# Loading a quarter of each query block first, and a highway pass by 128-column chunks, in a top-32 attention kernel

## The chip, the cores and the metric

The kernel runs on one core of a Trainium2 chip. The metric is the device time of one execution in microseconds; the median of three runs before the change is 874.89 us (874.78 to 874.94).

The core's engines work side by side, each through its own list of instructions in order, and wait for each other by semaphores: PE (matrix multiplication and transposes), DVE (vector work, here the search for the largest scores), ACT (activations and copies out of PSUM), POOL (vector work on SBUF) and SP (which issues most transfers). PE writes to PSUM, which has 8 banks of 512 fp32 columns; SBUF holds everything else.

## The reference, cut to what matters

```python
# q, k, v: batch 8, 8 heads, sequence 576, head dimension 64, float32
scores = scale * np.matmul(q, k.transpose(0, 1, 3, 2))
kth = np.partition(scores, -32, axis=-1)[..., -32:-31]
scores = np.where(scores >= kth, scores, -1e9)
attn = np.exp(scores - scores.max(-1, keepdims=True))
attn = attn / (attn.sum(-1, keepdims=True) + 1e-9)
x = np.matmul(attn, v)            # then heads side by side: 4608 rows of 512
H = np.maximum(x @ w_h, 0.0)      # highway pass
T = 1.0 / (1.0 + np.exp(-(x @ w_t + b_t)))
out = T * H + (1.0 - T) * x
```

Each of the 36,864 score rows (8 x 8 x 576) of 576 elements keeps its 32 largest.

## The kernel before

**Tiles and groups.** The 576 rows of a head are cut into four interleaved quarters of 128 (row 4p + j is row p of quarter j) and a rest of 64. A group is one quarter (or the rests) of all 8 heads of a batch; it holds four pairs of tiles, each 128 query rows by 576 scores of two heads (the rest: two pairs of four heads). There are 144 pairs in all. Batch 0 starts with its quarter 0, heads 0 and 1.

**One pair's way.** `scores` (L186) multiplies the transposed queries with the transposed keys into the PSUM tile `ps` of four banks, of which there is one. `evac` (L206) lets ACT write relu(ps) into `z`. `tree` (L217) lets DVE take `hi`, the larger of each two of the 576 scores: the first half is read from `ps`, the second from `z`, so `ps` is free for the next pair only when `hi` is done. After each second pair, `folds` (L232) halves `hi` into `hh` and `h`, and `minima` (L252) lets POOL keep the smaller ones. `lists` and `lists_rest` (L338, L352) find the 32nd largest with DVE's MAX8 and MATCH_REPLACE8, the bulk of its work. `mask` (L376) lets ACT write a penalty `pen` for all scores below that; `parts` (L425) lets PE transpose scores and penalty into `zt` (four 128-chunks of one head) and `zr` (the last chunk of both heads, made by `ends`), and ACT take the exponential `et`; `av` (L456) multiplies by the values and ACT copies the sums out as `xs`. `norm` (L490) divides.

**Highway pass.** Per group, `ffn_x` transposes x into `xT`, `ffn_h` and `ffn_t` multiply with the two weights, and DVE, POOL and accumulating transfers combine the results.

**Order.** The main loop (L892) goes over steps n: `tree(n)`, folds after odd n, mask of pair n - 4, values of pair n - 5, scores of pair n + 1, lists. The engines' instructions are pinned to this written order (`Pinned`, L25); so are the DMAs issued with `ops.nc.queue`, while those issued with `nc.sync` are placed on SP's queue by a scheduler. The preparation of the next batch (its loads and transposes, `begin`, L802) is spread over the steps from 17 pairs before its first.

**The opening (L832 to L856).** For each pair of heads hp, `load` (L105) brings a block of keys `kin` and one of queries `qin`, all four quarters, in two transfers of 128 KB; `load_rest` (L116) brings the rests of all heads. `turn` (L138) transposes a block with four PE transposes into a PSUM bank `kqps` and copies it to `kq`, on ACT or, where `vec` is set, on DVE. Banks come from `ztps` (two) or from `fps` (one, tag "fp"). `turn_rest` (L157) does the same for the rests. Before scores(0) come: 12 idle transposes (`spin`), turn of kin 0, 3 spins, turn of qin 0 (copied by DVE), turn_rest of pair 0. In steps 0 to 2, the blocks hp = n + 1 are turned before scores(n + 1). DVE so has the copies of q blocks 0 and 1 among its first four instructions.

**The end (L979 to L1025).** Below, m is the third pair from the end, gp the group before the last, gl the last. The end is written out by hand: gp's highway pass, transposes and exponentials of pairs m + 1 and m + 2, then `values(m + 1)`, the last `zt`, and `values(m + 2)`. Then the highway pass of gl: one reciprocal over all heads and x in two halves (`norm`), four transposes and `xT` in two halves (`final_x`), `ffn_h` (hps), `ffn_d`, the judge, and `final_t` and `final_o` in two halves of 256 columns. The judge (L865 to L880) reduces flags that say whether a slower exact path has to run: `judge_lists` and `judge_scales` over the whole kernel's lists and reciprocals, `judge` over the partitions, by a PE transpose `bps`.

Of the kernel before, what the change touches and what calls it, by code (L numbers as in the profile page):

```python
# [8 lines left out]
AF = mybir.ActivationFunctionType  # L9
ALU = mybir.AluOpType  # L10
# [57 lines left out]
class Ops:  # L68
# [36 lines left out]
    def load(self, pr, name, hp, eng=None, other=None):  # L105
        nc, D, P = self.nc, self.D, self.P
        eng = eng or nc.sync
        t = self.ldpool.tile([P, J, 2, D], FP32, tag=name, name=name)
        src = pr[name[0]](2 * hp, 2 * hp + 2, 0, J * P)
        for hh in range(2):  # L110
            (other if other and hh else eng).dma_start(
                t[:, :, hh, :], src[hh].rearrange("(p j) d -> p j d", j=J)
            )
        pr[name, hp] = t

    def load_rest(self, pr, name, eng=None):  # L116
        t = self.ldpool.tile([self.R, self.H, self.D], FP32, tag=name, name=name, bufs=1)
        (eng or self.nc.sync).dma_start(
            t[:], pr[name[0]](0, self.H, J * self.P, self.S).rearrange("h p d -> p h d")
        )  # L120
        pr[name] = t
# [16 lines left out]
    def turn(self, pr, name, hp, bank=None, vec=False):  # L138


        nc, P = self.nc, self.P
        t = pr.pop((name, hp))
        pool, tag = (self.ztps, "zt") if bank else (self.fps, "fp")
        kqps = pool.tile([P, 512], FP32, tag=tag, name="kqps")
        for c in range(J):
            nc.tensor.transpose(
                kqps[:, c * P : (c + 1) * P],
                t[:, c, :, :].rearrange("p h d -> p (h d)"),
                self.ident[:],
            )  # L150
        dst = pr["kq"][:, "kq".index(name[0]), hp, 0 : J * P]
        if vec:
            nc.vector.tensor_copy(dst, kqps[:])
        else:
            nc.scalar.copy(dst, kqps[:])

    def turn_rest(self, pr, h0, h1):  # L157


        nc, R = self.nc, self.R  # L160
        kqps = self.fps.tile([self.P, 512], FP32, tag="fp", name="kqps")
        view = kqps[:].rearrange("p (i h r) -> p i h r", i=2, r=R)
        for i, name in enumerate(("krest", "qrest")):
            for hp in range(h0, h1):
                nc.tensor.transpose(
                    view[:, i, hp, :],
                    pr[name][:, 2 * hp : 2 * hp + 2, :].rearrange("p h d -> p (h d)"),
                    self.ident[0:R, 0:R],
                )
        nc.scalar.copy(  # L170
            pr["kq"][:, :, h0:h1, J * self.P : self.S], view[:, :, h0:h1, :]
        )
# [44 lines left out]
    def tree(self, n):  # L217
# [3 lines left out]
        if n % 2 == 0:  # L221
# [5 lines left out]
        ps = self.st[n].pop("ps")  # L227
        nc.vector.tensor_tensor(
            hi[:, half, :], ps[:, :, 0:H1], self.st[n]["sc"][:, :, H1:S], ALU.max
# [271 lines left out]
    def norm_x(self, g):  # L501
# [8 lines left out]
        for hs in (slice(0, H // 2), slice(H // 2, H)) if g.final else (slice(0, H),):  # L510
            made = (nc.vector if g.final else nc.gpsimd).tensor_tensor(
                x3[:, hs, :],
                xs3[:, hs, 0:D],
                rinv[0:ql, hs].unsqueeze(2).to_broadcast([ql, hs.stop - hs.start, D]),
                ALU.mult,
            )
# [6 lines left out]
    def final_x(self, g):  # L523


        nc, P, n_g = self.nc, self.P, self.n_g
        g.xT = self.fpool.tile([P, n_g, P], BF16, tag="xT", name="xT")
        g.xh = self.fpool.tile([P, self.dm], FP32, tag="xh", name="xh")
        half = n_g // 2
        for i0 in (0, half):  # L530
            xtps = self.ztps.tile([P, 512], FP32, tag="zt", name="xtps")
            for i in range(half):
                nc.tensor.transpose(
                    xtps[:, i * P : (i + 1) * P],
                    g.x[:, (i0 + i) * P : (i0 + i + 1) * P],
                    self.ident[:],
                )
            src = xtps[:, 0 : half * P].rearrange("p (g j) -> p g j", j=P)
            dst = g.xT[:, i0 : i0 + half, :]
            if i0:  # L540
                nc.scalar.mul(dst, src, 0.5)
            else:
                nc.vector.tensor_scalar_mul(dst, src, 0.5)
        nc.scalar.mul(g.xh[:], g.x[:], -0.5)

    def final_t(self, g, banks):
# [4 lines left out]
        g.tp = [b[:, 0:W] for b in banks]  # L551
        for j, tp in enumerate(g.tp):
            cs = slice(j * W, (j + 1) * W)
            for i in range(n_g):
                nc.tensor.matmul(
                    tp, g.xT[:, i, :], self.wt[:, i, cs],
                    start=(i == 0), stop=False,
                )
            nc.tensor.matmul(
                tp, self.cst[:], self.bt[:, cs], start=False, stop=True  # L560
            )
            nc.scalar.activation(tp, tp, AF.Tanh)
# [126 lines left out]
def kernel(  # L689
# [65 lines left out]
    with ExitStack() as cm:  # L755
# [78 lines left out]
        for name in ("kin", "qin"):  # L834
            ops.load(pr, name, 0, queue, nc.scalar)
        for name in ("krest", "qrest"):
            ops.load_rest(pr, name, queue)
        for hp in (1, 2):
            for name in ("kin", "qin"):
                ops.load(pr, name, hp, queue)  # L840
# [8 lines left out]
        spin(3)  # L849
        ops.turn(pr, "qin", 0, True, True)  # L850
        ops.turn_rest(pr, 0, 1)
        for name in ("kin", "qin"):
            ops.load(pr, name, 3, queue)
        ops.load_values(pr, queue)
        ops.scores(0, *pairs[0], preps[0])
        ops.evac(0)  # L856
        ffn = []
        step = 0
        ok = const([P, 4], FP32, "ok")
        bad = const([P, 4], FP32, "bad")  # L860
# [10 lines left out]
        def judge_scales():  # L871
            vec.tensor_reduce(ok[:, 2:3], scales[:], op=ALU.min, axis=AX.XY)
            vec.tensor_scalar(bad[:, 2:3], ok[:, 2:3], FAINT, None, ALU.is_lt)
            vec.tensor_reduce(bad[:, 3:4], bad[:, 0:3], op=ALU.max, axis=AX.X)

        def judge():
            bps = ops.zrps.tile([P, 512], FP32, tag="zr", name="bps")
            ops.nc.tensor.transpose(bps[0:1, 0:P], bad[:, 3:4], ident[:])
# [13 lines left out]
        while step <= NPR:  # L892
            n = step
            if have(n):
# [3 lines left out]
                if n + 1 < NHP:  # L898
                    for name in ("kin", "qin"):
                        ops.turn(  # L900
                            pr, name, n + 1, True, n == 0 and name == "qin"
                        )
                    if n == 0:
                        ops.turn_rest(pr, 1, NHP)
# [95 lines left out]
        ops.ffn_d(gp, ops.ffn_t(gp))  # L1000
        part, ends = ops.parts(m + 1)
# [4 lines left out]
        ends()  # L1006
        part, ends = ops.parts(m + 2, banks[3])
        part(0)
        ends()
        ops.ffn_e(gp)  # L1010
        ops.ffn_o(gp, *out_rows(gp))
        values(m + 1)
        part(1)
        judge_lists()
        values(m + 2)
        ops.norm(gl)
        ops.final_x(gl)
        judge_scales()
        ops.spare = [ops.fps.tile([P, 512], FP32, tag="fp", name="hps")]
        ops.ffn_h(gl)  # L1020
        ops.ffn_r(gl)
        ops.ffn_d(gl)
        judge()
        ops.final_t(gl, banks[0:2])
# [76 lines left out]
```

## Time and profile before

| | us |
|---|---|
| median of 3 runs | 874.89 |
| the profiled execution, its own time | 874.66 |
| its span, from the first instruction to the last | 872.9 |
| DVE busy | 843.6 |
| PE busy | 707.8 |
| ACT busy | 695.9 |
| POOL busy | 690.8 |
| first hi of DVE starts | 10.56 |
| second hi starts | 14.55 |
| first fold (hh) starts | 15.35 |
| last list maximum of DVE starts (two of them, 0.56) | 853.97 |
| last xs copied | 861.18 |
| last o of the highway pass ends | 868.23 |

How to read it: an engine's list is one line per instruction or run of like instructions: start, duration, engine, line, operation, what is written from what, count, and in brackets how long the engine was idle before it and whose end let it go on. All kernel instructions that go through `Pinned` show its line, L35, so they are told apart by the names of their tiles. The chain of waits follows the last instruction back to what released it. DVE's instructions and their waits decide here; the granted clock of PE is given as a share of full speed.

### The profile page before, as it was taken

To read this page: it belongs to the slowest core of one execution; us is meant where nothing else is said; L and a number is where in the kernel's file an instruction comes from. 1 tells how busy PE (TensorE), PEld (TensorE's weight loads), DVE (VectorE), ACT (ScalarE), POOL (GpSimd) and SP (SyncE) were. 2 spreads that over 40 slices of the span, in tenths; PEclk is the share of its full clock that TensorE was granted. 3 is DMA by queue.
4 is the path that set the end of the run, shared out by engine and by line. 5 is a ranking of instruction groups with operands and counts; after the bars stand their busy time and mean duration, and the time that the engine had idled before them with its cause. 6 is when DMAs were issued, how large, how long until landed. Compare 5 with 4: busy or idle time off the path is not lost.

```text
span 872.9 us, 19884 instructions
## 1 busy us (share of the span) xinstructions
PE 707.8 (81%) x6569; PEld 500.4 (57%) x6569; DVE 843.6 (97%) x4200; ACT 695.9 (80%) x1244; POOL 690.8 (79%) x447
## 2 busy tenths in 40 slices
PE   6777988879788788778788798887978878887975
PEld 5455655655565555655565565665556655555653
DVE  4999999999999999999999999999999999999995
ACT  3788878888788887888888887888878888677784
POOL 5788887888878888888888888878888888877880
PEclk9799999999999998999999999999989999899898
DMA  9553422234234331323323432323412111111111
GB/s 196 130 110 62 109 38 57 60 62 98 37 62 92 73 86 29 70 67 62 86 50 56 96 80 56 62 64 69 105 37 46 42 37 38 37 26 25 26 39 38
DMA packets 104494, 57.06 MB, mean 65 GB/s; under 512 B 82112, under 2 KB 91712, under 8 KB 104384
## 3 DMA queue, kind: packets, MB, share of 16 engines
q1 hardware_dynamic: 92768, 37.37, 17.0%
q0 software_dynamic: 10416, 17.96, 13.6%
q8 instruction: 53, 0.87, 0.4%
q14 instruction: 57, 0.47, 0.2%
q10 hardware_dynamic: 1200, 0.39, 0.2%
HBM read 30.67 MB, written 17.30 MB: 55 GB/s over the span
## 4 chain that ended last, share of the span: by engine, by line
DVE 90%; PE 4%; POOL 2%; DMA 1%; issue 1%; ACT 1%; SPq 0%; DVEq 0%; POOLq 0%; ACTq 0%
DVE w L35 48%; DVE m L35 18%; DVE hi L35 11%; DVE hh L35 6%; DVE h L35 4%; DVE d L35 3%; PE ps L35 1%; POOL hi L35 1%; PE zt L35 1%; POOL hh L35 1%; PE t L35 1%; DMA d<-xh 1%; DMA qrest<-in_q_dram 1%; PE zr L35 1%; ACT z L35 1%
## 5 line engine op out<-in xcount | busy, mean ns | idle before, releaser
L35 PE MATMUL ps<-kq 64*128 64x64 f32 (+3 forms) x1280 | 212.1, 457 | 89.5 <-DVE hi L35 85.4
L35 ACT ACTIVATE z<-ps 128x1152 f32<-128x1152 f32 x144 | 163.0, 1132 | 103.5 <-PE ps L35 101.2
L35 ACT ACTIVATE pen<-z,m 128x576 bf16<-128x576 f32 x288 | 225.9, 785 | 1.3 <-DVE m L35 1.1
L35 PE MATMUL zt<-ident,z 128*128 128x128 f32 x1152 | 225.7, 289 | 0.1
L35 PE MATMUL zt<-nident,pen 128*128 128x128 bf16 x1152 | 215.0, 225 | 0.3 <-ACT pen L35 0.3
L35 PEld LDWEIGHTS ps<-kq 64*128 64x128 f32 (+1 forms) x1280 | 107.5, 184 | 187.6 <-DVE hi L35 96.1
L35 POOL TENSOR_TENSOR hi<-z,hi 128x1152 int32<-128x1152 int32 x72 | 189.3, 2630 | 14.7 <-DVE m L35 9.2
L35 POOL TENSOR_TENSOR hh<-hi,hh 128x576 int32<-128x576 int32 x71 | 100.2, 1411 | 126.3 <-DVE w L35 126.3
L35 POOL TENSOR_TENSOR hi<-hi,z 128x1152 int32<-128x1152 int32 x72 | 190.3, 2643 | 5.7
L35 PEld LDWEIGHTS zt<-ident,z 128*128 128x128 f32 x1152 | 169.9, 147 | 19.1 <-ACT xT L35 0.6
L35 ACT ACTIVATE et<-zt 128x512 bf16<-128x512 f32 x288 | 161.5, 606 | 14.1 <-PE zt L35 13.3
L35 PEld LDWEIGHTS <-pen 128*128 128x128 bf16 x1440 | 160.0, 111 | 1.7 <-ACT pen L35 1.7
L35 DVE MAX8 m<-w 128x8 f32<-128x168 f32 x576 | 160.4, 320 | 0.0
L35 DVE MAX8 w<-hi 128x8 f32<-128x288 f32 x288 | 116.7, 447 | 0.0
L35 DVE TENSOR_TENSOR hi<-ps,z 128x576 f32<-128x576 f32 x144 | 106.8, 741 | 6.5 <-ACT z L35 6.5
L35 PE MATMUL zr<-v,et 128*128 128x65 bf16 (+1 forms) x1590 | 89.6, 196 | 18.5 <-ACT et L35 14.6
L35 POOL TENSOR_TENSOR hh<-hh,hi 128x576 int32<-128x576 int32 x71 | 100.0, 1408 | 5.6
L35 PEld LDWEIGHTS <-et 128*128 128x128 bf16 (+1 forms) x1600 | 69.8, 101 | 60.0 <-ACT et L35 46.0
L35 DVE MATCH_REPLACE8 w<-m,w 128x168 f32<-128x168 f32 x288 | 89.4, 318 | 0.0
L35 DVE MAX8 w<-hh 128x8 f32<-128x72 f32 x576 | 84.3, 221 | 0.0
L35 PE MATMUL zr<-ident,z 128*128 128x128 f32 x286 | 74.2, 313 | 3.5 <-ACT xs L35 3.5
L35 PE MATMUL zr<-nident,pen 128*128 128x128 bf16 x286 | 59.8, 230 | 0.3 <-ACT pen L35 0.3
(91 smaller groups left out, 1111.6 us busy)
## 6 DMA issues: line engine op xcount, KB each, us to landing
vin<-in_v_dram SPq DMA_DIRECT2D x8, 1024.0 KB, 5.6
kin<-in_k_dram SPq DMA_DIRECT2D x63, 128.0 KB, 3.4
qin<-in_q_dram SPq DMA_DIRECT2D x63, 128.0 KB, 3.1
out_dram<-x SPq DMA_DIRECT2D x30, 256.0 KB, 2.8
d<-xh POOLq DMA_DIRECT2D x30, 256.0 KB, 3.8
out_dram<-d POOLq DMA_DIRECT2D x30, 256.0 KB, 4.4
krest<-in_k_dram SPq DMA_DIRECT2D x8, 128.0 KB, 4.2
qrest<-in_q_dram SPq DMA_DIRECT2D x8, 128.0 KB, 5.0
```

What stands on the lines that cost most here:

```text
L35: return self._tc.keep_in_program_order(fn(*args, **kw))
```

## The change

There are three parts.

1. **Opening.** Scores of the first group need only quarter 0 of each query block. A new `load_first` brings that quarter for heads 0 and 1, and then for heads 2 to 7, into a tile `qc`; `turn_first` transposes it (one transpose per pair of heads) and DVE copies it to `kq`. The rest of the query blocks is loaded later, without that quarter (`c0=1`), and turned in steps 3 to 6, on the single fps bank with ACT copies of 128x384; the query rests are loaded from step 4 and turned in step 8. `krest` comes in two pieces, the first on ACT's queue. Keys are turned one step earlier: kin 1 before the first step, and kin n + 2 in step n, ahead of scores(n + 1) on PE and ACT. The 3 spins are gone. As the q blocks share three buffers, and the query rests one, with those of batch 1, SP's order of loads changes: the query rest of batch 1 is now loaded before that of batch 0.
2. **First maxima.** For the first four pairs `tree` reads both operands from `z`; `ps` is free when ACT has evacuated it.
3. **End.** The highway pass of the last group runs in column chunks as pairs of heads end: chunks 0 and 1 (heads 0 to 3) are normalised and transposed while gp's pass and the last pairs are still at work, chunks 2 and 3 follow one by one, and hps and the two t tiles accumulate chunk by chunk, with the bias first. The scaled copy `xh` goes to POOL but for the last chunk. The last `zt` goes ahead of `values(m + 1)`. `judge_scales` comes early and `judge_last` checks the last group's reciprocals.

The diff, cut to its core:

```diff
-    def load(self, pr, name, hp, eng=None, other=None):
+    def load(self, pr, name, hp, eng=None, other=None, c0=0):
...
-                t[:, :, hh, :], src[hh].rearrange("(p j) d -> p j d", j=J)
+                t[:, c0:J, hh, :],
+                src[hh].rearrange("(p j) d -> p j d", j=J)[:, c0:J, :],
...
+    def load_first(self, pr, eng, h0, h1):
+        if not h0:
+            pr["qc"] = self.ldpool.tile(
+                [self.P, self.H, self.D], FP32, tag="qc", name="qc", bufs=1
+            )
+        src = pr["q"](h0, h1, 0, J * self.P)
+        eng.dma_start(
+            pr["qc"][:, h0:h1, :],
+            src.rearrange("h (p j) d -> p h j d", j=J)[:, :, 0, :],
+        )
+
+    def turn_first(self, pr, h0, h1):
+        nc, P = self.nc, self.P
+        kqps = self.ztps.tile([P, 512], FP32, tag="zt", name="kqps")
+        for hp in range(h0, h1):
+            nc.tensor.transpose(
+                kqps[:, hp * P : (hp + 1) * P],
+                pr["qc"][:, 2 * hp : 2 * hp + 2, :].rearrange("p h d -> p (h d)"),
+                self.ident[:],
+            )
+        nc.vector.tensor_copy(
+            pr["kq"][:, 1, h0:h1, 0:P],
+            kqps[:, h0 * P : h1 * P].rearrange("p (h q) -> p h q", q=P),
+        )
...
-    def turn(self, pr, name, hp, bank=None, vec=False):
+    def turn(self, pr, name, hp, bank=None, c0=0):
...
-        for c in range(J):
+        for c in range(c0, J):
...
-        ps = self.st[n].pop("ps")
+        ps, sc = self.st[n].pop("ps"), self.st[n]["sc"]
+        if n < 4:
+            ps = sc
         nc.vector.tensor_tensor(
-            hi[:, half, :], ps[:, :, 0:H1], self.st[n]["sc"][:, :, H1:S], ALU.max
+            hi[:, half, :], ps[:, :, 0:H1], sc[:, :, H1:S], ALU.max
         )
...
+    def final_norm(self, g, i0, i1):
+        nc, P, D = self.nc, self.P, self.D
+        hs = slice(2 * i0, 2 * i1)
+        xs3 = g.xs[:].rearrange("p (h e) -> p h e", e=D + 1)
+        rinv = self.scales[:, g.gi, hs]
+        nc.vector.reciprocal(rinv, xs3[:, hs, D])
+        nc.vector.tensor_tensor(
+            g.x[:].rearrange("p (h d) -> p h d", d=D)[:, hs, :],
+            xs3[:, hs, 0:D],
+            rinv.unsqueeze(2).to_broadcast([P, 2 * (i1 - i0), D]),
+            ALU.mult,
+        )
+
+    def final_turn(self, g, i0, i1, xtps):
+        nc, P = self.nc, self.P
+        for i in range(i0, i1):
+            nc.tensor.transpose(
+                xtps[:, (i - i0) * P : (i - i0 + 1) * P],
+                g.x[:, i * P : (i + 1) * P],
+                self.ident[:],
+            )
...
+        if i1 - i0 == 1 and i1 < self.n_g:
+            nc.scalar.mul(dst, src, 0.5)
+        else:
+            nc.vector.tensor_scalar_mul(dst, src, 0.5)
+        if i1 == self.n_g:
+            nc.scalar.mul(g.xh[:, cs], g.x[:, cs], -0.5)
+        else:
+            nc.gpsimd.tensor_scalar_mul(g.xh[:, cs], g.x[:, cs], -0.5)
...
-        for name in ("kin", "qin"):
-            ops.load(pr, name, 0, queue, nc.scalar)
-        for name in ("krest", "qrest"):
-            ops.load_rest(pr, name, queue)
-        for hp in (1, 2):
-            for name in ("kin", "qin"):
-                ops.load(pr, name, hp, queue)
+        ops.load(pr, "kin", 0, queue, nc.scalar)
+        ops.load_rest(pr, "krest", nc.scalar, 0, 2)
+        ops.load_first(pr, queue, 0, 2)
+        ops.load(pr, "kin", 1, queue)
+        ops.load_first(pr, queue, 2, H)
+        ops.load_rest(pr, "krest", queue, 2, H)
+        ops.load(pr, "kin", 2, queue)
...
         spin(12)
         ops.turn(pr, "kin", 0, True)
-        spin(3)
-        ops.turn(pr, "qin", 0, True, True)
-        ops.turn_rest(pr, 0, 1)
-        for name in ("kin", "qin"):
-            ops.load(pr, name, 3, queue)
+        ops.turn_first(pr, 0, 1)
+        ops.turn_rest(pr, 0, 1, ("krest",))
+        ops.load(pr, "kin", 3, queue)
+        ops.load(pr, "qin", 0, queue, None, 1)
         ops.load_values(pr, queue)
+        ops.load(pr, "qin", 1, queue, None, 1)
+        ops.load(pr, "qin", 2, queue, None, 1)
         ops.scores(0, *pairs[0], preps[0])
         ops.evac(0)
+        ops.turn_first(pr, 1, NHP)
+        ops.turn(pr, "kin", 1, True)
+        ops.turn_rest(pr, 1, NHP, ("krest",))
...
-                if n + 1 < NHP:
-                    for name in ("kin", "qin"):
-                        ops.turn(
-                            pr, name, n + 1, True, n == 0 and name == "qin"
-                        )
-                    if n == 0:
-                        ops.turn_rest(pr, 1, NHP)
+                if n + 2 < NHP:
+                    ops.turn(pr, "kin", n + 2, True)
+                if NHP <= n + 1 < 2 * NHP:
+                    ops.turn(pr, "qin", n + 1 - NHP, None, 1)
+                if n == NHP:
+                    ops.load(pr, "qin", 3, None, None, 1)
+                    ops.load_rest(pr, "qrest")
+                if n == 2 * NHP:
+                    ops.turn_rest(pr, 0, NHP, ("qrest",))
...
         ops.ffn_d(gp, ops.ffn_t(gp))
+        ops.final_begin(
+            gl, ops.fps.tile([P, 512], FP32, tag="fp", name="hps"), banks[1:3]
+        )
...
+        ops.final_norm(gl, 0, 2)
+        ops.ffn_e(gp)
+        ops.ffn_o(gp, *out_rows(gp))
+        ops.final_turn(gl, 0, 2, banks[0])
         part, ends = ops.parts(m + 2, banks[3])
         part(0)
         ends()
-        ops.ffn_e(gp)
-        ops.ffn_o(gp, *out_rows(gp))
+        judge_lists()
+        judge_scales()
+        part(1)
         values(m + 1)
-        part(1)
-        judge_lists()
+        ops.final_norm(gl, 2, 3)
         values(m + 2)
-        ops.norm(gl)
-        ops.final_x(gl)
-        judge_scales()
-        ops.spare = [ops.fps.tile([P, 512], FP32, tag="fp", name="hps")]
-        ops.ffn_h(gl)
-        ops.ffn_r(gl)
+        ops.final_h(gl, 0, 2)
+        ops.final_turn(gl, 2, 3, ...)
+        ops.final_norm(gl, 3, 4)
+        ops.final_t(gl, 0, 2)
+        ops.final_turn(gl, 3, 4, ...)
+        ops.final_h(gl, 2, 3)
+        ops.final_t(gl, 2, 3)
+        judge_last(gl)
+        ops.final_h(gl, 3, 4)
         ops.ffn_d(gl)
+        ops.final_t(gl, 3, 4)
         judge()
-        ops.final_t(gl, banks[0:2])
         ops.final_o(gl, out_rows(gl), (nc.sync, ops.nc.scalar))
```

`final_h` and `final_t` are `ffn_h` and the old `final_t` for chunks i0 to i1; `final_t` puts the bias matmul first and the tanh after the last chunk.

## The prediction

> **What bounds the kernel now.** I read the page's busy line and slices first, then what DVE waited for, then the opening and the tail instruction by instruction.
>
> ```profile
> PE 707.8 (81%) x6569; PEld 500.4 (57%) x6569; DVE 843.6 (97%) x4200; ACT 695.9 (80%) x1244; POOL 690.8 (79%) x447
> DVE  4999999999999999999999999999999999999995
> ```
>
> DVE is busy 97%, at 9 in every slice but the first and the last. So 29.3 us (872.9 - 843.6) is all that any change can win without taking work off DVE, and it should lie at the ends. The waits of DVE say where:
>
> ```profile
> DVE kq L35 <- PE kqps L35: 7.2, 1, 7.2
> DVE hi L35 <- ACT z L35: 6.5, 4, 2.6
> DVE scales L35 <- ACT xs L35: 2.8, 1, 2.8
> ```
>
> 7.2 us before the first copy, 6.5 us before first maxima (hi), 2.8 us before the last reciprocal. Between 60 and 850 us the same view has one wait of 0.4 us. Now the opening, from the timeline:
>
> ```profile
> 8.06 1.30 PE L35 MATMUL ps<-kq 64*128 64x512 f32 x8
> 9.39 1.13 ACT L35 ACTIVATE z<-ps 128x1152 f32<-128x1152 f32 x1 [0.91 <-PE ps L35]
> 10.56 0.76 DVE L35 TENSOR_TENSOR hi<-ps,z 128x576 f32<-128x576 f32 x1 [2.64 <-ACT z L35]
> ...
> 12.06 1.30 PE L35 MATMUL ps<-kq 64*128 64x512 f32 x8 [0.71 <-DVE kq L35]
> ...
> 14.55 0.76 DVE L35 TENSOR_TENSOR hi<-ps,z 128x576 f32<-128x576 f32 x1 [2.64 <-ACT z L35]
> 15.35 0.76 DVE L35 TENSOR_TENSOR hh<-hi 128x576 f32<-128x576 f32 x1
> ```
>
> From 15.35 DVE runs without a gap, but for 0.84 us before the fourth hi (23.05). So the opening is worth what the start of the folds (hh, 15.35) moves, plus that 0.84. Scores(0) waits for qrest (issued 3.09, landed 4.8 later, 7.89); scores(1) waits for DVE's copy of the second q block (11.23 to 11.91), which stands behind the first hi. The tail, from the chain of waits:
>
> ```profile
> 859.14 0.73 PE zt L35 x8
> 859.87 0.02 issue
> 859.89 0.60 ACT et L35
> ...
> 860.91 0.28 ACT xs L35
> ...
> 861.58 0.43 DVE x L35
> ...
> 863.08 1.48 PE hps L35 x4
> 864.55 0.21 PE bps L35
> 864.77 2.15 PE t L35 x10
> ...
> 867.80 0.43 DVE o L35
> ```
>
> From the last xs (ends 861.18) to the last o (ends 868.23) lie 7.05 us of serial highway pass in one piece. After it the store and the program's end take 4.7 us, which nothing here changes.
>
> **The opening, part by part.** Loads: all these DMAs move 256-byte pieces, and the issues with their times to landing give the rate: the first half of k block 1 landed at 8.27 (3.77 + 4.5) as byte 896 KB of the queue, the first half of q block 2 at 11.86 (7.96 + 3.9) as 1664 KB, so 214 GB/s, 0.6 us per 128 KB; early ones were 256 KB by 4.16 (k block 0) and 512 KB by 6.22 (q block 0). I place the new order on this line by cumulated bytes: k block 0 4.16 as before; with the first qc piece (64 KB) and krest of two heads (32 KB, on ACT's queue, same bytes) 352 KB: 4.16 + 96/256 x 2.06 = 4.9 to 5.7; k block 1 (608 KB) 6.8; other qc (800 KB) 8.0; other krest (896 KB) 8.3; k block 2 (1152 KB) 9.5; qrest of batch 1, which SP now issues here, 1280 KB; k block 3 (1536 KB) 11.3; the rest of q block 0 12.2; vin some 4 us later, about 17 instead of 19.3.[...]
>
> Scores(0): k block 0 is transposed 4.26 to 5.35 as before; then one qc transpose and one krest, 0.27 each: 5.9 to 6.2; DVE's 128x128 copy, between 0.2 and the 0.69 of the 512-wide one, takes about 0.3 and ACT's 64-wide one 0.2 (0.27 at 128): scores(0) at 6.3 for 8.06. With the 1.30 to 1.6 for them, z(0) runs 7.8 to 8.95. DVE must then copy the other qc (landed 8.0, three transposes to 8.45, copy 0.55 by 384/512 of 0.69) to 9.05 before the first hi, which so starts at 9.1. That copy is a new thing in front of hi, but z(0) hides all but 0.1 of it.
>
> Scores(1) now stands behind k blocks 1 and 2 on PE: block 2 landed 9.5, four transposes 0.66: 10.2. ACT's copies in front of it (k block 1 from 9.1, 0.58; krest, 0.35) end 10.1. It no longer waits for hi(0), as ps is free when z(0) ends. Scores(1) 10.2 to 11.5, z(1) to 12.7, hi(1) to 13.5: folds at 13.5, **1.85 us earlier**. hi from z instead of ps costs nothing: 128x576 takes 0.758 from SBUF (hh<-hi) and 0.741 from ps.
>
> Then z(2) is ready at 15.8 and DVE wants it at 17.15 (13.5 + 3.67 as now). Scores(3) starts when z(2) ends (15.9) instead of when hi(2) ends (19.9); even in 2.40 us z(3) ends 19.45, wanted at 20.35: the **0.84 us** go too.
>
> **What is moved into the steady part.** Steps 3 to 6 each get three transposes (0.5 on PE) and a 128x384 ACT copy (0.45), step 8 the qrest turn (0.4 PE, 0.3 ACT). All use the single fp bank, so from step 5 on PE waits there until ACT has copied batch 1's block out (35.40 to 35.98 for the first), and values(0) and the next scores queue behind it: 0.7 wait + 0.45 + 0.5 put z(6) about 1.1 later. Now z(5), z(6), z(7) end 1.14, 1.63 and 2.19 us before hi wants them (34.34, 40.13, 45.64). That fits, narrowly; below it costs nothing, above, with PE slow, up to 1.2. I take 0.3. The qrest load waits for batch 1's turn_rest (one buffer): issued about 44.2, landed 47.4, PE there about 47.5, hi(8) 48.7, so hidden with some 2 us to spare.
>
> **The tail, part by part** (times as if the rest stood still). Heads 0 to 3 are complete with the xs at 854.66: reciprocal 0.2 and x 0.42 on DVE after 855.12, in the 0.67 us in which DVE now waits for the tanh; PE's two transposes at 856.7 (0.4), while it waits for pen until 857.23; xT (0.42) to 857.6. Free. xh goes to POOL: 1.27 for a 512-wide pair op bounds it above; POOL is idle from 857.97 and xh is wanted at 863, so any price hides.
> The judge's reductions (1.80 + 0.27 + 0.48 + 0.15) follow on DVE to 860.3, where it now idles to 861.21.
> Values(m+1) go behind the last zt on PE: zt starts at 858.45 instead of 858.94, and xs(m+1) leaves ACT's path, so et ends 859.95 (860.49) and the last xs 860.7 (861.18): 0.5 gained. DVE: pair 2's reciprocal 860.3, x (its 0.17 gap, then 0.28 for 128 columns, between 0.2 and 0.42) to 860.95; pair 3's to 861.6.
> PE: two hps (0.52 of the 1.04 that four take at full clock) to 861.0; transpose; six 256-wide t at 0.13 to 862.05; last transpose to 862.3; chunk 2's three 0.52; xT of chunk 3 on DVE (0.28) to 862.65; its hps 863.0 and t 863.3. DVE: judge_last (three small ones and gaps, 0.6; two of them are new) 863.25; d 0.69; flag 0.45 to 864.4; then d, o, d, o of 0.42 each with gaps, ending 866.18 instead of 868.23. **2.05 us.** Fully at half clock PE's part is 1.2 longer: 0.9.
>
> **The clock speaks against parts of this.** The windows:
>
> ```profile
> 20.00:25.00 5.00, 2.99 (x12) 1.64 (x14) 4.09 (x22) 1.13 (x1) 3.15 (x2) 0.54 0.84 175
> 863.00:866.00 3.00, 2.92 (x12) 1.68 (x13) 1.74 (x7) 0.90 (x3) 0.00 (x0) 0.59 0.00 0
> ```
>
> Granted 0.54 and 0.59: in the first the same scores took 2.39 for 1.30, in the second four hps 1.48 for 1.04. The Trainium skill (TensorE: Matmul & The Clock Gate, "What's actually happening") says that full clock is granted only after a free-running window of some 3.4 us found PE busy, and is lost after an idle one. By that rule, taking 3 spins and four q blocks' transposes from the opening makes PE idler and could leave it slow sooner or longer: scores(0) at half clock puts the folds 0.6 to 1.1 later (gain 0.75 to 1.25), and a slow window over scores(6) brings out the 1.2. By the rows, 12 spins and k block 0 fill PE from 1.59 on as now; z(2) and z(3) have 0.9 to spare at half clock. I go with the rows, and let the rule set the 0.3 and the upper end. In the tail the rule favours the change: PE has less idle time between 860 and 863.
>
> **Sum.** Span 872.9 - 1.85 - 0.84 + 0.3 - 2.05 = 868.5. The profiled execution took 874.66, 1.76 over its span: 870.2. It lies 0.23 under the median 874.89: **870.4 us**, 0.5% faster.
>
> **Rivals.**
> (a) The steady part eats the opening: the fp bank and a slow window make z(6) and z(7) late, 1.2 and about 0.8. For it: the 1.14 and 1.63 us of slack. Against: DVE lost nothing at 25 to 60 us even with 2.4 us scores. 872.1.
> (b) The tail stays serial: PE at half clock through it, or DVE's judge work (to 860.3) holding pair 2 back: gain 0.9 instead of 2.05: 871.5. For it: DVE has only 0.3 us of slack there.
> (c) It does nothing at the start, qc landing as late as qrest did (7.9): the folds move by 0.3 only, the 0.84 stays won: 872.0. Against: it is byte 352 KB, not 768.
> (d) Slower: PE loses the full clock in the opening and does not get it back. At half clock its 4.8 us of a 5.8 us step become 9 or so, PE is the bound, and every window of 3.4 us costs DVE some 1.3 to 1.7. It decides from the third window beyond today's four slow ones (20.4 to 34.1); five are slower by 0.2%: 877. Against: the second slice of the whole span and all later ones show 0.9 and above after the same sparse opening.
>
> **How the numbers follow.** A measurement of this kernel tells about 0.2% (1.75 us) from no change. Forecast as summed 0.58, own range 869.3 to 871.3; (a) 0.14, (b) 0.13, (c) 0.06, (d) 0.04, and 0.05 for a gain larger than forecast (all best ends: folds 2.3, tail 2.6: 869.0). Low 868.9 takes the last; high 872.6 takes (a), (b), (c) with their spread, leaving (d) and two rivals together. Same needs 873.1 or more, two rivals at once: 0.06; slower 0.04; faster 0.90.
>
> **What would show it.** Right: first hi near 9.1, folds near 13.5, no DVE wait before the fourth hi, hi without waits at 25 to 60 us, last o some 5.5 us after the last xs, which comes 0.5 nearer to the last list maximum. Wrong: DVE hi waiting for ACT z at 30 to 50 us with PE at kqps before it; granted clock 0.5 in more than four windows before 40 us; PE waiting for qc beyond 6; d of the last group waiting for hps or xh beyond 863.3.

## The result: no difference, and the profile after

| | before | after |
|---|---|---|
| median, same chip, us | 874.84 (4 runs, 874.04 to 874.94) | 875.65 (4 runs, 874.83 to 876.04) |
| ratio, 95% interval | | 1.001 (0.9993 to 1.0027) |
| profiled execution, us | 874.66 | 875.56 |
| its span, us | 872.9 | 873.7 |

The forecast was 870.4 us, 868.9 to 872.6. The change made the kernel neither faster nor slower. Both ends did gain, though. The table cuts the two spans at the same events, taken from the timelines (starts of DVE's instructions; the ends of the last xs and the last o):

| stretch, us | before | after | difference | predicted |
|---|---|---|---|---|
| start to first fold (hh) | 15.35 | 13.04 | -2.31 | -1.85 |
| first fold (hh) to fifth hi | 13.49 | 13.95 | +0.46 | -0.84 |
| fifth to eleventh hi | 34.00 | 39.88 | +5.88 | +0.3 |
| eleventh hi to last list maximum | 791.13 | 790.36 | -0.77 | 0 |
| to the last xs | 7.20 | 6.79 | -0.41 | -0.5 |
| to the last o | 7.05 | 4.81 | -2.24 | -1.55 |
| to the end | 4.67 | 4.91 | +0.24 | 0 |

So 5.9 us were lost between 27 and 67 us, in a stretch where DVE had no wait in the kernel before. (The -0.77 further down is what single executions differ by: that stretch took 790.3 to 791.4 us in all the profiled kernels.) The busy line and the slices of DVE hardly show it (845.2 us, and 9 in every slice but three):

```profile
PE 702.5 (80%) x6566; PEld 496.0 (57%) x6566; DVE 845.2 (97%) x4206; ACT 696.2 (80%) x1247; POOL 693.4 (79%) x449
DVE  5979999999999999999999999999999999999996
```

The 7 in the third slice (44 to 66 us) is the one trace of it. DVE's waits name it (us in total, times, longest):

```profile
DVE kq L35 <- PE kqps L35: 7.4, 2, 5.4
DVE scales L35 <- ACT xs L35: 5.3, 1, 5.3
DVE hi L35 <- ACT z L35: 3.4, 2, 3.0
```

Before, the wait of scales (2.8 us) was the last reciprocal, in the tail. This one of 5.3 us is another. In the timeline it begins at 52.78, where DVE has finished its list replacements and the next thing in its order is the reciprocal of group 0:

```profile
52.57 0.21 DVE L35 MATCH_REPLACE8 w<-m,h 128x72 f32<-128x72 f32 x1
58.10 0.20 DVE L35 RECIPROCAL scales<-xs 128x8 f32<-128x8 f32 x1 [5.32 <-ACT xs L35]
58.22 0.59 DVE L35 MAX8 w<-w 128x8 f32<-128x72 f32 x4
```

The maxima at 58.22 need no xs; they stand behind the reciprocal. Where xs comes from is in the chain of waits between 45 and 58 us (start, us, what):

```profile
45.13 10.90 DMA qrest<-in_q_dram
56.04 0.14 issue
56.17 0.66 PE kqps L35 x4
56.83 0.66 PE zr L35 x10
57.49 2.33 PE ps L35 x8
```

PE stands before the turn of batch 0's qrest until its load has landed. Behind it in PE's order are values(3) (the ten zr) and scores(9) (ps), and from zr comes the xs. In the windows, PE does nothing at all from 50 to 55 us, and the DMA engines are at 1.01 and 1.08 of their time (columns: window, its length, busy us of PE, PEld, DVE, ACT, POOL, granted clock, DMA share, GB/s):

```profile
45.00:50.00 5.00, 3.77 (x34) 2.70 (x32) 4.96 (x18) 4.54 (x9) 4.45 (x6) 1.00 1.01 151
50.00:55.00 5.00, 0.00 (x0) 0.00 (x0) 2.78 (x19) 0.00 (x0) 4.54 (x2) 0.78 1.08 185
55.00:60.00 5.00, 3.83 (x25) 2.52 (x26) 1.90 (x17) 1.97 (x5) 1.04 (x1) 0.54 0.15 33
```

The same windows of the kernel before, which the prediction does not show, have the DMA engines at 0.72 and 1.19 while DVE loses nothing:

```profile
45.00:50.00 5.00, 3.70 (x42) 2.90 (x38) 4.93 (x19) 3.98 (x8) 4.52 (x7) 1.00 0.72 120
50.00:55.00 5.00, 3.24 (x36) 2.36 (x33) 5.00 (x29) 3.20 (x6) 4.84 (x3) 1.00 1.19 205
```

The opening in the timeline of the kernel after:

```profile
9.74 1.30 PE L35 MATMUL ps<-kq 64*128 64x512 f32 x8
11.08 1.13 ACT L35 ACTIVATE z<-ps 128x1152 f32<-128x1152 f32 x1 [0.65 <-PE ps L35]
12.24 0.76 DVE L35 TENSOR_TENSOR hi<-z 128x576 f32<-128x576 f32 x1 [3.05 <-ACT z L35]
13.04 0.76 DVE L35 TENSOR_TENSOR hh<-hi 128x576 f32<-128x576 f32 x1
...
15.60 2.62 POOL L35 TENSOR_TENSOR hi<-z,hi 128x1152 int32<-128x1152 int32 x1 [6.82 <-DVE m L35]
...
16.72 2.12 DVE L35 TENSOR_TENSOR hi<-z 128x576 f32<-128x576 f32 x1
...
18.30 3.03 POOL L35 TENSOR_TENSOR hi<-hi,z 128x1152 int32<-128x1152 int32 x1
...
21.19 0.75 DVE L35 TENSOR_TENSOR hi<-z 128x576 f32<-128x576 f32 x1
```

The folds start at 13.04, and the fourth hi (21.19) has no wait in front of it, as forecast. But the third hi took 2.12 us instead of 0.75. It started inside POOL's operation (15.60 to 18.22) and ended 0.62 us after that one's end. The tail in the chain of waits:

```profile
860.55 0.49 ACT et L35
...
863.37 0.34 PE t L35 x5
863.70 0.45 PE hps L35 x2
864.15 0.29 PE xtps L35
864.44 0.66 PE t L35 x6
...
866.18 0.69 DVE d L35
...
868.39 0.42 DVE o L35
```

Nothing is serial in one piece any more: half of hps (0.45) runs before the last chunk's x, and six t (0.66) before the last chunk's transpose. PE also kept its full clock there, granted 1.00 where the kernel before had 0.59:

```profile
863.00:866.00 3.00, 2.79 (x26) 1.57 (x22) 1.94 (x10) 1.21 (x5) 0.53 (x1) 1.00 0.00 0
```

### The profile page after: what moved, and what is told of

It reads as the page before. It is cut to its first block, busy times and chain, and to the rows that moved or that the text cites. A ratio compares the mean times of both kernels' runs of the same rounds, so it can differ in the third digit from the quotient of the medians.

```text
span 873.7 us, 19892 instructions
## 1 busy us (share of the span) xinstructions
PE 702.5 (80%) x6566; PEld 496.0 (57%) x6566; DVE 845.2 (97%) x4206; ACT 696.2 (80%) x1247; POOL 693.4 (79%) x449
## 3 DMA queue, kind: packets, MB, share of 16 engines
q0 software_dynamic: 10416, 17.96, 13.2%
## 4 chain that ended last, share of the span: by engine, by line
DVE 91%; PE 3%; ACT 2%; DMA 2%; issue 1%; SPq 1%; DVEq 0%; ACTq 0%
DVE w L35 49%; DVE m L35 19%; DVE hi L35 11%; DVE hh L35 6%; DVE h L35 4%; DVE d L35 3%; DMA qrest<-in_q_dram 1%; PE ps L35 1%; ACT et L35 1%; PE zt L35 1%; ACT pen L35 1%; SPq L35 1%; ACT z L35 1%; DVE scales L35 0%; DMA kin<-in_k_dram 0%
## 5 line engine op out<-in xcount | busy, mean ns | idle before, releaser
L35 PE MATMUL ps<-kq 64*128 64x64 f32 (+3 forms) x1280 | 215.1, 462 | 88.3 <-DVE hi L35 84.2
L35 PE MATMUL zt<-ident,z 128*128 128x128 f32 x1152 | 220.6, 285 | 0.0
L35 PE MATMUL zt<-nident,pen 128*128 128x128 bf16 x1152 | 210.4, 223 | 0.1
L35 PEld LDWEIGHTS zt<-ident,z 128*128 128x128 f32 x1152 | 166.8, 145 | 17.0
L35 PEld LDWEIGHTS <-pen 128*128 128x128 bf16 x1440 | 157.9, 110 | 2.3 <-ACT pen L35 2.0
L35 DVE TENSOR_TENSOR hi<-ps,z 128x576 f32<-128x576 f32 x140 | 103.4, 738 | 0.4 <-ACT z L35 0.4
```

Of the source, the lines that this page charges most:

```text
L35: return self._tc.keep_in_program_order(fn(*args, **kw))
```

## The experiments

Two things were to be explained: the 5.3 us at 52.78, and the third hi. All kernels of one series ran on one chip beside the kernel before. Single executions of one kernel there lie up to 4.8 us apart (no_lock: 869.02 to 873.86), so ratios are given with their intervals, and the stretches of the table above are used where one event is in question.

### What the turn of qrest costs, and why its load is late

**own_buffer**

```diff
@@ load_rest
-    def load_rest(self, pr, name, eng=None, h0=0, h1=None):
+    def load_rest(self, pr, name, eng=None, h0=0, h1=None, tag=None):
...
-                [self.R, self.H, self.D], FP32, tag=name, name=name, bufs=1
+                [self.R, self.H, self.D], FP32, tag=tag or name, name=name, bufs=1
@@ opening
         ops.load(pr, "qin", 2, queue, None, 1)
+        ops.load_rest(pr, "qrest", queue, tag="qrest0")
@@ loop, n == NHP
-                    ops.load_rest(pr, "qrest")
```

> One edit to the changed kernel: batch 0's qrest gets a buffer of its own and is loaded in the opening behind the third q block, so that it waits for no turn of batch 1; its turn stays at step 8. Theory A (PE stands 7.3 us at the turn of qrest, whose load was issued at 45.1 and landed at 56.0; values(3) and DVE's reciprocal of group 0 stand behind it): the turn runs at about 48.9, the 5.3 us wait of the reciprocal and the 0.37 us of the next hi are gone, 875.6 - 5.7 = 869.9 us, between 869 and 871. Theory B (the loss comes from the three q blocks' turns on the single fp bank in steps 3 to 6, which make z late): the reciprocal's wait moves to hi, and the time stays at 874 to 876.

Measured: 870.9 us, ratio 0.9961 (0.9948 to 0.9974), span 869.1. DVE has no wait of scales, and the fifth to the eleventh hi take 34.01 us, the 34.00 of before. Theory A holds, B falls: the three q blocks still go through the one fp bank, and no hi waits for z from the third on to the eleventh. The second batch's load of qrest now goes out at 44.76 and takes 9.4 us to land, nearly as slow; nobody waits for it.

**turn_later**

```diff
-                if n == 2 * NHP:
+                if n == 3 * NHP:
                     ops.turn_rest(pr, 0, NHP, ("qrest",))
```

> One edit to the changed kernel: the turn of batch 0's qrest moves from step 8 to step 12; the load stays where it is, late and slow. Theory A says that only the place of the waiting turn in PE's queue costs: qrest lands at about 56, PE is at step 12 near 70, so nothing waits, 869.9 us (869 to 871). Theory B: 874 to 876. If it lands between, a part of the loss is the load itself taking DMA time from others.

Measured: 870.34 us, ratio 0.9956 (0.9943 to 0.9969), span 868.6; fifth to eleventh hi 34.31. DVE's waits in the first 62 us:

```profile
DVE kq L35 <- PE kqps L35: 7.9, 2, 5.5
DVE hi L35 <- ACT z L35: 3.1, 2, 2.9
```

The waits for kqps and 2.92 of the 3.1 us of hi belong to the opening. The other 0.22 stand before the seventh hi (38.75), and there the q blocks' turns do show: PE was granted 0.61 from 30 to 35 us, for 0.83 in own_buffer, and z came late (the kernel before, without these turns, had 0.59 there and no wait). The load is still slow: issued at 45.91, it landed 8.6 us later. Moving the instruction that waits for it by four steps gives 5.57 of the 5.88 us back.

**weights_later**

```diff
-            if n == 5:
+            if n == 8:
                 load_weights()
```

> One edit to the changed kernel: the loads of wh, wt and bt (1152 KB, issued at 43.25 to 45.0 in step 5) move to step 8; qrest's load stays. It tells whether qrest took 10.9 us because of these or for its place behind batch 1's turn. Theory A1 (the weights hold the DMA engines): qrest lands some 5 us after 45.1, as the median of its eight loads (4.9), PE waits about 1 us at the turn, the xs of values(3) end near 52, before DVE is there at 52.8: no wait, 870 us (869.5 to 871.5). Theory A2 (the load is late and slow by itself): it still lands past 54, 874 to 876.

Measured: 871.96 us, ratio 0.9973 (0.9962 to 0.9984), span 868.9; fifth to eleventh hi 34.78, no wait of scales. The tile's own view gives the time from issue to landing, here over two loads of qrest in this stretch:

```profile
L123 SPq DMA_DIRECT2D qrest<-in_q_dram x2: 618/620/622, 45.1 to 50.2; - x2
DMA to landing us min/median/max: 3.3/3.4/3.4
```

Issued at the same 45.1, with no weights under way, qrest lands after at most 3.4 us instead of 10.9. So A1 holds: the 1152 KB of wh, wt and bt, issued by POOL from 43.25 to 45.0, delay it. The time is 0.5 us above the expected range, and the median is above those of the two other repairs, though the intervals overlap. The trace shows 0.85 us of this: behind the issues of the weights, POOL's x (56.86 to 58.10) now runs while DVE folds, and the fold w<-hh at 57.12, with two SBUF inputs, takes 1.30 instead of 0.45 us, to 0.32 after POOL's end. Below, the third hi has the same trouble.

### The two parts alone

**tail_alone** has the kernel before with the change's functions `final_begin` to `final_t`, `judge_last` and the order of the tail; **opening_alone** has the rest of the change with the tail of before.

> The kernel before with the tail's change alone (the opening as before). The prediction's sum says 2.05 us: 874.84 - 2.05 = 872.8; its rival (b), a tail that stays serial, says 0.9: 873.9. The trace of the changed kernel has the last o 11.6 us after the start of the last list maximum where the one before has 14.3, which says 2.7: 872.2.

Measured: 872.16 us, ratio 0.9978 (0.9967 to 0.9988): 1.9 us by the ratio. Last list maximum to last xs 6.67 us, from there to the last o 4.82, together 2.76 less than before. The sum's 2.05 lies in the interval (1.0 to 2.9 us); the 0.9 of rival (b) lies just outside it.

> The kernel before with the opening's change alone (loads of a quarter, first maxima from SBUF, qrest late), the tail as before. The tail alone gave 874.25 to 872.16 on its chip, 2.1 us. If the parts add up, the opening alone is 875.6 + 2.1 to 2.7 = 877.7 to 878.3 us, slower than before by 3 us, of which 5.7 are the qrest load. If the opening alone is at 875 or less, something in the changed tail undoes a part of it, and the account of the trace is incomplete.

Measured: 878.4 us, ratio 1.0047 (1.0031 to 1.0063). The opening alone makes the kernel slower, by 4.1 us by the ratio and 3.6 by the medians, as expected (the range is missed by 0.1). Its folds start at 12.99, and the fifth to the eleventh hi take 39.54. The parts add up: 0.9978 x 1.0047 = 1.0025, within the interval of the change.

### Why the third hi takes 2.12 us

The rest is built on turn_later.

**sbuf_two, sbuf_none, sbuf_eight**

```diff
-        if n < 4:
+        if n < 2:
             ps = sc
```

with 0 and 8 in the place of 2.

> The kernel turn_later (qrest turned at step 12) with one more edit: only the first two maxima (n below 2 instead of 4) read z twice from SBUF; the third and the fourth read ps again. Theory P (an operation of DVE with both inputs in SBUF stands still while POOL works on SBUF: the third hi started 1.1 us into POOL's 2.62 us one and ended 0.62 us after it): the third hi takes 0.75 instead of 2.12 us. Against it, scores(3) must again wait for that hi: z(3) is ready at 19.0 to 21.2 by the clock, where DVE wants it at 20.0, so 0 to 1.2 us of wait come back before the fourth. Net 0.2 to 1.3 us gained on 870.3: 869.0 to 870.1 us. Theory Q (the 2.12 us has to do with ACT or a DMA at that moment, not with the source): the third hi stays near 2 us, and the time rises by up to 1.2.

Measured: 870.96 us, ratio 0.9962 (0.9949 to 0.9975).

```profile
18.14 0.75 DVE L35 TENSOR_TENSOR hi<-ps,z 128x576 f32<-128x576 f32 x1
...
21.38 1.13 ACT L35 ACTIVATE z<-ps 128x1152 f32<-128x1152 f32 x1 [5.23 <-PE ps L35]
22.55 0.76 DVE L35 TENSOR_TENSOR hi<-ps,z 128x576 f32<-128x576 f32 x1 [1.23 <-ACT z L35]
```

The third hi is back at 0.75, inside POOL's operation (17.02 to 19.63), and the fourth waits 1.23 us again. First fold to fifth hi: 13.89 us, for 13.96 in turn_later. The stall and the wait are worth the same, and the gain that was expected is not there. Theory P holds, its sum does not.

> turn_later with all first maxima reading ps, so without the second part of the change. By theory P: the third hi takes 0.75. hi(0) ends before scores(1) can start, so that costs nothing; scores(2) and scores(3) wait for hi(1) and hi(2), and z(3) is late by 0 to 1.2 us as in sbuf_two: 869.0 to 870.3 us, no slower than turn_later, so that reading SBUF was worth nothing. If reading SBUF is needed, there are waits of more than 1.4 us before hi, and it is over 870.5.

Measured: 870.63 us, ratio 0.9961 (0.9947 to 0.9975); first fold to fifth hi 13.88, with 1.23 us of waiting before the fourth hi. The time is 0.3 us over the expected range, but the stretch is that of turn_later (13.96): reading SBUF for the first maxima brought nothing that these runs show.

> turn_later with eight instead of four first maxima reading z twice from SBUF: the dose of theory P. In turn_later POOL runs its 128x1152 pair while DVE does the fifth and the seventh hi (26.6 to 29.3 beside 27.0, 38.0 to 40.6 beside 38.3, by the changed kernel's trace), not the sixth and the eighth. P: the fifth and seventh take 2.8 to 3.0 us, the sixth and eighth 0.75, span up by 4.3 us to 873. Q: all four take 0.75, and the span stays at 868.6.

Measured: 875.22 us, ratio 1.0014 (1.0004 to 1.0024), 4.9 us over turn_later in the medians (on another chip); span 874.2, of which 1.35 is a later first fold.

```profile
28.51 2.90 DVE L35 TENSOR_TENSOR hi<-z 128x576 f32<-128x576 f32 x1
36.20 0.75 DVE L35 TENSOR_TENSOR hi<-z 128x576 f32<-128x576 f32 x1
...
41.98 2.91 DVE L35 TENSOR_TENSOR hi<-z 128x576 f32<-128x576 f32 x1
...
28.17 2.63 POOL L35 TENSOR_TENSOR hi<-z,hi 128x1152 int32<-128x1152 int32 x1
30.88 3.05 POOL L35 TENSOR_TENSOR hi<-hi,z 128x1152 int32<-128x1152 int32 x1
41.63 2.64 POOL L35 TENSOR_TENSOR hi<-z,hi 128x1152 int32<-128x1152 int32 x1
```

The fifth and the seventh hi end 0.61 and 0.62 us after POOL's operation (30.80 and 44.27); the sixth, with POOL idle, takes 0.75. Theory P holds, Q falls.

**hi_first**

```diff
             if have(n):
-                ops.tree(n)
+                if n != 2:
+                    ops.tree(n)
...
                 if n == 1:
+                    ops.tree(2)
                     opening = ops.lists(0, *pairs[0])
```

> turn_later with one more edit: the third hi (the first maxima of pair 2, both inputs z in SBUF) is issued in step 1, ahead of the list maxima m that POOL's first 128x1152 pair waits for, so that it runs before POOL starts. The source stays SBUF and scores(3) stays early. Theory P (DVE waits for POOL's operation to end): the third hi takes 0.75 instead of 2.12 us, z(3) then ends about 0.3 us after DVE wants it, so from the first fold to the fifth hi it is 12.6 to 13.0 us instead of 13.96. About 1 us under turn_later: 869.3 us. Theory Q (reading z twice from SBUF is slow for the third pair wherever it stands): 13.9 and no gain.

Measured: 870.19 us, ratio 0.995 (0.9938 to 0.9962), and 13.93 us from the first fold to the fifth hi. P's mechanism held and its sum failed:

```profile
15.28 0.75 DVE L35 TENSOR_TENSOR hi<-z 128x576 f32<-128x576 f32 x1
19.73 2.12 DVE L35 TENSOR_TENSOR hi<-z 128x576 f32<-128x576 f32 x1
...
15.52 3.00 POOL L35 TENSOR_TENSOR hi<-z,hi 128x1152 int32<-128x1152 int32 x1 [6.70 <-DVE hh L35]
18.59 2.64 POOL L35 TENSOR_TENSOR hi<-hi,z 128x1152 int32<-128x1152 int32 x1
```

The third hi, issued 0.24 us before POOL's operation, took 0.75, and it was POOL that took 3.00 instead of 2.62. But with DVE 1.4 us ahead the fourth hi fell into POOL's second operation (to 21.23) and ended 0.62 after it. The stall had moved on by one instruction.

**k2_behind, hi_first_k2, no_lock** were to beat both kernels: k block 2 is turned behind scores(1), alone (with n below 2), with hi_first (n below 4), and with hi_first and n below 3.

```diff
-                if n + 2 < NHP:
+                if n == 1:
                     ops.turn(pr, "kin", n + 2, True)
...
                 ops.evac(n + 1)
+                if n == 0:
+                    ops.turn(pr, "kin", n + 2, True)
```

> sbuf_two with one more edit, meant to beat both kernels: k block 2 is turned behind scores(1) instead of in front of it, with its copy behind z(1) on ACT. In turn_later scores(1) started at 9.91 although its last input was copied at 9.44, because block 2's transposes (9.36, after 0.44 us of waiting for its load) stood in front. Expected: scores(1) at 9.5, the folds some 0.4 us earlier, 0.4 us under sbuf_two; scores(2) then waits for block 2's copy behind z(1) (to 12.6 instead of 12.4), which z(2) can bear. 868.6 to 869.7 us. If z(2) or z(3) get late instead, no gain.

Measured: 870.69 us, ratio 0.996 (0.9946 to 0.9974). First hi at 8.58 and folds at 12.37, where turn_later has 8.74 and 13.21: the step gains 0.7 there, more than expected. It does not show in the median, which is 1.0 us above the expected range. In the profiled execution 1.0 us is lost again from the last list maximum to the last xs (7.68 for 6.67), after a window with a granted clock of 0.50 from 846 to 849 us (0.96 in turn_later).

> hi_first and the edit of k2_behind together (k block 2 turned behind scores(1); the first four maxima read SBUF): meant to beat both kernels. In k2_behind the folds started 0.84 us earlier than in turn_later. Expected: first fold near 12.4, from there 12.6 to 13.2 us to the fifth hi, span 867.0 to 867.6, 868.7 to 869.3 us. If z(2) comes after DVE wants it (first fold + 2.4), a part of it is lost.

Measured: 869.66 us, ratio 0.995 (0.9937 to 0.9963), span 867.3; folds at 12.39, but 13.93 from there to the fifth hi, as in hi_first and for the same reason: the fourth hi takes 2.12. The time is 0.4 us above its range.

> hi_first_k2 with one more edit: the fourth hi reads ps (n below 3 instead of 4 from SBUF); in hi_first_k2 it started at 19.18 inside POOL's 128x1152 pair (18.04 to 20.68) and took 2.12 us, ending 0.61 us after it. Theory P: it takes 0.75, as ps is in PSUM; the third, issued 0.24 us before POOL's pair, keeps 0.75 and POOL's pair keeps 3.0. From the first fold to the fifth hi 12.5 to 12.7 us instead of 13.93, span near 865.9, 867.7 to 868.4 us, the fastest of all. If the fourth hi stays at 2.1 us, P is wrong.

Measured: 869.99 us, ratio 0.9959 (0.9945 to 0.9972), span 867.2, first fold to fifth hi 13.11 instead of the 12.5 to 12.7 expected; the time, too, is above its range, by 1.6 us.

```profile
19.01 0.74 DVE L35 TENSOR_TENSOR hi<-ps,z 128x576 f32<-128x576 f32 x1
19.78 1.32 DVE L35 TENSOR_TENSOR hh<-hi 128x576 f32<-128x576 f32 x1
...
17.86 2.62 POOL L35 TENSOR_TENSOR hi<-hi,z 128x1152 int32<-128x1152 int32 x1
```

The fourth hi is back at 0.74, and now the fold behind it, which also reads SBUF twice, waits: it ends 0.62 us after POOL (20.48). Of the 1.37 us, 0.82 are won, and 0.56 went into hh. All repaired versions but sbuf_eight are faster than the kernel before, weights_later by 0.3% and the others by 0.4 to 0.5%; their intervals overlap, so no order among them is shown. The changed kernel did not run beside them, but its ratio, 1.001 (0.9993 to 1.0027), lies outside all their intervals.

## Why the prediction was wrong, step by step

**The step that failed** is "The qrest load waits for batch 1's turn_rest (one buffer): issued about 44.2, landed 47.4, PE there about 47.5, hi(8) 48.7, so hidden with some 2 us to spare." The wait for the buffer and the time of issue were right (45.13). The landing was not: it came 10.9 us after the issue instead of 3.2. The profile before gives 5.0 us as the median of these loads, has wh and wt issued in the same stretch (45.10 and 46.03, landing after 7.3 and 9.0 us), and shows what the load of batch 1's qrest, issued between the two, took there:

```profile
L118 SPq DMA_DIRECT2D qrest<-in_q_dram x1: 613/613/613, 45.2 to 45.2; - x1
DMA to landing us min/median/max: 6.5/6.5/6.5
```

weights_later shows 3.4 us without the weights. The consumer was wrong too: the prediction counts its cover of 2 us to hi(8), the first maxima of pair 8, while what stood behind the turn on PE was values(3), and behind its xs the reciprocal in DVE's order. This alone would have cost nothing. From the landing (56.03) to the reciprocal (58.10) went 2.07 us, so to be in time for 52.78 the load had about 5.6 us (an estimate from these times): with 3.2 some 2 us were indeed to spare, with 6.5 none. Cost of the 10.9: 5.32 us before the reciprocal and 0.37 before the next hi; turn_later and own_buffer give it back.

**"hi from z instead of ps costs nothing"** failed too. It rested on hh<-hi, 0.758 us, a row in which POOL was never in one of its long operations: in the kernel before, the folds run beside none of them, and hi, which does, reads ps. The prediction does not weigh the rule that speaks against this edit (first point of the last section). The 0.84 us before the fourth hi did go, and 1.37 came in the third: +0.46 instead of -0.84 by the stretch, and nothing either way by sbuf_none.

**The opening** was right in its mechanism and mis-sized by 0.46: scores(0) ran at 5.93 (forecast 6.3), the first hi at 8.44 (9.1), scores(1) at 9.74 (10.2), the folds at 13.04 (13.5). A part is chance: tail_alone, with the opening of before, has its folds at 14.79 for 15.35.

**The steady part's 0.3** was 0.0 in own_buffer and 0.3 in turn_later, by the fifth to eleventh hi. Its mechanism was right: z(6) ended 0.33 us before hi(6) wanted it, for 1.63 before, so it came 1.30 us later (the prediction writes 1.1, though the parts that it names add up to 1.65). Rival (a) is real only in small: hi(6) waited 0.22 us in turn_later, 0.39 in k2_behind and 0.18 in no_lock, and in no run the 1.2 and 0.8 that the rival has.

**The tail** was right and mis-sized: 2.65 us (2.76 in tail_alone) for 2.05. The last xs came 0.41 nearer to the last list maximum (0.5); d started 2.18 us after it (2.55 by the sum), the last o ended 2.63 after that (2.93). Six t took 0.66 us, 0.11 each where the sum has 0.13. What the prediction expected of the clock here came about: with PE busy 2.83 us instead of 1.08 from 860 to 863, the granted clock of the next 3 us was 1.00 instead of 0.59 (and 1.00 in tail_alone from 859 to 862). Rival (b) falls.

**Rivals (c) and (d)** fall: the first copy of qc ran at 5.40, and the clock was 0.76, 0.50 and 0.88 over 10 to 20, 20 to 30 and 30 to 40 us, against 1.00, 0.52 and 0.80 before. It did drop earlier (scores(3) took 1.97), and no hi was late for it; in turn_later, with the same opening, it was 1.00 over 10 to 20 us. The argument against (d) misreads its row, though: the second slice of the span is at 0.7, not 0.9, and five later ones are at 0.8.

```profile
PEclk9799999999999998999999999999989999899898
```

A smaller form of (d), scores(0) at half clock with folds 0.6 to 1.1 later, is real in some executions: see the last point below.

**The sum with what was measured**: 868.5 - 0.46 (opening) + 1.30 (first maxima) + 5.58 (qrest, less the 0.3) - 0.60 (tail) = 874.3; the steady part's -0.77 and the end's +0.24 make it 873.8, the span 873.7. Without the qrest step's loss the forecast ratio, 0.995, lies within the interval of turn_later: the other errors cancelled. That the outcome was no difference had been given 0.06, for two rivals at once. None of the rivals was of this kind; a wait newly placed in front of values(3) should have been one.

## What to carry to other kernels

When a load is made late, ask two things: what else is on the DMA engines at that time, and which instruction waits for it and what stands behind that one on its engine, down to the engine that sets the end. Moving the waiting instruction was as good here as moving the load. And a duration read from a row holds for what ran beside it: a DVE operation with two SBUF inputs had its 0.75 us here only when POOL was not at work on SBUF, and a stall taken from one such operation went to the next (hi_first, no_lock).

## What the runs showed of the hardware

- **DVE and POOL exclude each other where DVE reads SBUF twice.** A 128x576 operation of DVE that fell into one of POOL's long operations ended 0.61 to 0.62 us after POOL's end every time (2.12, 2.90, 2.91 and, for hh, 1.32 us instead of 0.75), while hi<-ps,z in the same place took 0.75. The Trainium skill says so (SBUF — State Buffer, "Who interferes with whom"): a DVE instruction with two SBUF inputs contends with a GpSimd one that reads SBUF, and the first to issue blocks the other. The runs agree in both directions: in hi_first DVE is first, and POOL takes 3.00 instead of 2.62. The fold of weights_later is half as large and ended 0.32 us after POOL's end.
- **A 128 KB load took 10.9 us beside 1152 KB of another queue**, and 3.4 us at most at the same time without them. This is no fixed price: loads of qrest at this place took 6.5 us in the kernel before, 8.6 in turn_later and 9.4 in own_buffer, and in the changed kernel the load of krest, issued 0.7 us ahead of the slow one, took 2.8.
- **PE's clock dropped after its 7.3 us of idling**: granted 0.54 from 55 to 60 us, and scores(9) took 2.37 us for the usual 1.30.
- **PE's speed at the very start differs between executions.** In the profiled executions of sbuf_two, sbuf_none and sbuf_eight scores(0) took 2.40 us, and the folds started at 14.4 to 14.6; in the other nine with the changed opening it took 1.30 to 1.59, and the folds started at 12.2 to 13.2. The 2.40 is what scores take at a granted clock near 0.5 (2.39 in the kernel before at 20 to 25 us, with 0.54), but the windows from 5 to 12 us show 1.00 in all of them, so it is the duration of the matmuls that tells. Why, and what decides it, was not found (the three ran on one chip, but so did k2_behind, with 1.30); a gain of 1 us in the opening is hard to see in single executions for this reason.
